# Order on ScalarE's queue: the clamp of w_out's third pair of pieces, the early up product's gelu, and the copies of the turned state reads

## The chip, the cores and the metric

The kernel runs on one core of a Trainium2 chip, in one launch. The metric is the device time in microseconds (us), the median of several runs. Engines are named as in the profile: PE is TensorE, DVE is VectorE, ACT is ScalarE, and PEld is TensorE's loading of weights.

## The reference

Block-recurrent cross attention (8 batches, 8 heads, 512 tokens, 32 state rows, 64 per head) is followed by a two-layer block with a quick gelu on 8 x 544 tokens, with a model width of 512 and an inner width of 2048. The weights w_in and w_out come as doubles, all else is float32.

```python
scores = scale * np.matmul(x, state.transpose(0, 1, 3, 2))
a = softmax(scores);   xread = np.matmul(a, state)
scores2 = scale * np.matmul(state, x.transpose(0, 1, 3, 2))
a2 = softmax(scores2); sread = np.matmul(a2, x)
x = concatenate([xread, sread], axis=2)      # then (B, H, S, D) -> (B*S, H*D)
h = x @ w_in
g = h * (1.0 / (1.0 + np.exp(-1.702 * h)))
return g @ w_out
```

## The kernel before

The order of every engine's work is written out by hand: an instruction is put on its engine's queue where the program calls for it, and semaphores settle the rest. Batches 0 and 1 are worked on together, while the weights come in; then the batches from 1 on take the steady route (`strassen_two`), each with the attention of the next one hooked in. Products with w_out use Strassen's seven products, P1 to P7.

**Rounding the weights.** w_in and w_out arrive in pieces (128 rows of 512 doubles, read as pairs of integer words), and are turned to float32 in pairs of pieces. A pair takes five steps on VectorE and two on ScalarE: the mask of the exponent bits (`pair_mask`, L305, into a part of `low`), the clamp of the exponents (`pair_clamp`, two relus on ScalarE in the same place, L225 and L226), the sign (L318, which reads the clamp's result), the low words (L319), the fraction (`pair_fraction`, L313), and the last product, which leaves the rounded pair in place (L322). `round_pair(j)` does the sign, the low words and the last product of pair j; `round_next(j)` slips the mask and the fraction of pair j + 1 between them, and then calls for the clamp of pair j + 1. Pairs 0 to 7 are w_in's, 8 to 15 are w_out's; pair 10 is w_out's third.

**The stage around the change.** It is the loop over eight slots i at the end of batch 0: in each slot the down products P1 to P7 of batch 0 gain one more part of their sums, from pair 8 + i. Their results stand in seven PSUM banks from the first slot to the last: P1, P6, P2 and P5 in the banks o_0 to o_3, P7 and P3 in the two banks of `psH`, and P4 in one of the two of `psA`. VectorE forms the sums of halves of w_out (`pair_sums`, into sums, t_room and w_out itself) and, in even slots, those of the activations (`left_sums`, into s_room). TensorE takes a slot's products in the order P1, P2, P6, P5, P7, P3, P4, each of four matmuls of 128x256; from the third slot on each slot also has one up product of batch 1 (four matmuls of 128x512) with its gelu (L659).

The first slot is different. After P1 it has the rest of batch 1's up matrices, the reads of the state by attention (`att_sread`), the sums of the first pair, `round_next(9)`, P2, one early up product of batch 1 (`up_x(1, f_early, dst=early)`, in a bank of `psH`, gelu to a room of xn, since its own room isn't free yet), the turning of the two batches' state reads (`att_srT`: a transpose on TensorE and a copy on ScalarE, L649, out of banks of `psA`), and P6, P5, P7, P3, P4. P3 is written to the bank that the early up product's gelu reads, and P4 to a bank that a copy of the turned state reads empties.

After the loop VectorE gathers the seven banks to batch 0's output (L1478, L1629) and makes sums that go out to DRAM (L1450). `strassen_two(1)` begins with P1 and P2 (L866), in between the scores of batch 2 (L456), which VectorE turns (L481); VectorE's first sum into osb (L873) frees the bank o_1 for the low-level products (L817), whose results ScalarE copies (L826).

Of the kernel before, what the change touches and what calls it, by code (L numbers as in the profile page):

```python
# [20 lines left out]
def kernel(  # L21
# [72 lines left out]
    def att_ps(shape, name):  # L94
        return psA.tile(shape, FP32, tag="att", name=name)
# [84 lines left out]
    PIECES = [("i", c, k) for c in range(NFC) for k in range(NPR)] + [("o", HF * k + (f + HF // 2) % HF) for f in range(HF) for k in range(2)]  # L180
# [43 lines left out]
    def clamp(sc):  # L224
        nc.scalar.activation(out=sc.bitcast(FP32), in_=sc, func=AF.Relu, bias=edge[0], scale=-8.0)  # L225
        nc.scalar.activation(out=sc, in_=sc.bitcast(FP32), func=AF.Relu, bias=edge[1], scale=-1.0)  # L226
# [67 lines left out]
    def pair_room(j):  # L294
        return low[:, 2 + 2 * j % 4 : 4 + 2 * j % 4].bitcast(I32)
# [7 lines left out]
    def pair_mask(j):  # L303
        load_weights(2 * j + 2)
        nc.vector.tensor_scalar(pair_room(j), pair_hi_lo(j)[0], 0x7FF00000, None, ALU.bitwise_and)  # L305

    def pair_clamp(j):
        clamp(pair_room(j))
        done["a"] = 2 * j + 2

    def pair_fraction(j):
        hi, _ = pair_hi_lo(j)
        nc.vector.tensor_scalar(pair_dst(j).bitcast(I32), hi, 0xFFFFF, 0x100000, ALU.bitwise_and, ALU.bitwise_or)  # L313

    def round_pair(j, *fills):
        hi, lo = pair_hi_lo(j)
        dst, sc = pair_dst(j), pair_room(j)
        nc.vector.scalar_tensor_tensor(sc, hi, -0x80000000, sc, ALU.bitwise_and, ALU.bitwise_or)  # L318
        nc.vector.scalar_tensor_tensor(dst, lo, 2.0**-32, dst.bitcast(I32), ALU.mult, ALU.add)  # L319
        for fn in fills:  # L320
            fn()
        nc.vector.scalar_tensor_tensor(dst, dst, 2.0**-20, sc.bitcast(FP32), ALU.mult, ALU.mult)  # L322
        done["b"] = 2 * j + 2
        raw.clear()
        refill()

    def round_next(j):
        round_pair(j, *((lambda: pair_mask(j + 1), lambda: pair_fraction(j + 1)) if 2 * j + 2 < len(PIECES) else ()))
        if 2 * j + 2 < len(PIECES):
            pair_clamp(j + 1)  # L330

    def piece(fill):
# [263 lines left out]
    def att_M(b, c, spare=False, banks=None, copied=True):  # L596

        m = mpool.tile([P, NG, FC], FP32, tag=f"M{turns['M'] % NFC if b < 2 else c}", name=f"M_{b}_{c}")
        turns["M"] += 1
        A[b]["M", c] = m  # L600
        name = f"M_{b}_{c}_"
        ps = banks or [
            psH.tile([P, FC], FP32, tag="h", name=name + str(g)) if spare else att_ps([P, FC], name + str(g)) for g in range(NG)
        ]
        by_state(b, ps, lambda rows, j: w_in[c][rows, j])
        M_banks[b, c] = ps
        if copied:
            M_copies(b, c)
# [15 lines left out]
    def eT_turn(b, g):  # L624
        t = A[b]["eT"][:, g].rearrange("p c q -> p (c q)")
        nc.vector.transpose(t, t)

    def att_sread(b):

        a = A[b]  # L630
        ps = att_ps([P, NG, D], f"sr_{b}")
        for g in range(NG):
            for c in range(SCH):
                for j in range(NPR):
                    st = slice(Ns * j, Ns * (j + 1))
                    e, v = a["eT"][:, g, j, Ns * c : Ns * (c + 1)], xn[b][:, NG * j + g, c]
                    nc.tensor.matmul(  # L637
                        ps[st, g], e, v,
                        start=(c == 0), stop=(c == SCH - 1),
                    )  # L640
        sr = apool.tile([P, P], FP32, tag="sr", name=f"sr_{b}", bufs=2)
        for g in range(NG):
            nc.scalar.activation(out=sr[:, D * g : D * (g + 1)], in_=ps[:, g], func=AF.Copy, scale=a["e2"][g][1])
        A[b]["sr"] = sr

    def att_srT(b):
        ps = att_ps([P, P], f"srT_{b}")
        nc.tensor.transpose(ps, A[b]["sr"], ident)
        nc.scalar.copy(srT[:, :, b, :], ps.rearrange("p (j n) -> p j n", j=NPR))  # L649
# [6 lines left out]
    def gelus(n):  # L656
        for _ in range(n):
            fn, kw = waiting.pop(0)
            fn(**kw)  # L659
# [728 lines left out]
    nin = NFC * NPR  # L1388
# [81 lines left out]
    def pieces(t, *shape):  # L1470
        n, k = shape
        return t.rearrange("p a b -> p (a b)").rearrange("p (n k t) -> p n k t", n=n, k=k)
# [17 lines left out]
    def a_of(f):  # L1490
        lo, hi = G[0, f // 2][:, f % 2], G[0, (HF + f) // 2][:, f % 2]
        return lo[:, :HS], hi[:, :HS], lo[:, HS:], hi[:, HS:]

    def t24(i):
        return t_room[i // 2][:, i % 2] if i < HF // 2 else T24[:, ORDER[i]]

    def turns_of(*lists):

        for step in zip(*lists):
            for fn, args in step:  # L1500
                fn(*args)

    def s_of(i):
        return tuple(v[:, i % 4] for v in s_rooms)

    def left_sums(i):

        u = ORDER[i] // 2
        (a11, a21), (a12, a22) = quarters(0, u, S), quarters(0, HF // 2 + u, S)
        s1, s2, *s4 = (v[:, i % 4 : i % 4 + 2] for v in s_rooms)  # L1510
        return [(tt, v) for v in ((s1, a21, a22, ALU.add), (s2, s1, a11), (a21, a11, a21), *((s, a12, s2) for s in s4))]
# [18 lines left out]
    def pair(i, *names):  # L1530

        f = ORDER[i]
        a11, a12, a21, a22 = a_of(f)
        s1, s2, s4 = s_of(i) if i >= 0 and names[0] not in ("P1", "P2") else (None,) * 3
        t = t24(i) if s1 is not None else None
        for name in names:
            lhs, rhs = {
                "P1": lambda: (a11, B11[:, f]),
                "P2": lambda: (a12, B21[:, f]),
                "P5": lambda: (s1, T1[:, f]),  # L1540
                "P6": lambda: (s2, t[:, 0]),
                "P7": lambda: (a21, B12[:, f]),
                "P3": lambda: (s4, B22[:, f]),
                "P4": lambda: (a22, t[:, 1]),
            }[name]()
            for r in range(2):
                nc.tensor.matmul(  # L1547
                    ps7[name][:, HN * r : HN * (r + 1)], lhs[:, P * r : P * (r + 1)], rhs,
                    start=(i == 0 and r == 0), stop=(i == HF - 1), skip_group_check=True,
                )  # L1550
# [10 lines left out]
    for i in range(HF):  # L1561
        if i > 1:
            round_next(nin // 2 + i)
        gelus(len(waiting))
        if i == 3:
            nc.scalar.copy(G[1, f_early // 2][:, f_early % 2], early)
        if i == 0:
            pair(i, "P1")
            att_M(1, 2, banks=bank_o[1::2])
            att_M(1, 3, True)  # L1570
            for b in (1, 0):
                for g in range(NG):
                    eT_turn(b, g)
            turns_of(left_sums(0))
            for b in (1, 0):
                att_sread(b)
            t_room.append(pieces(apool.tile([P, NG, SCH * P], FP32, tag="eT", name="t_room_1"), 2, 2))
            s_rooms.append(four(apool.tile([P, NG, NB * Ns], FP32, tag="e1", name="s4_room")))
            pair_sums(i, left_sums(0)[3:])
            round_next(nin // 2 + 1)  # L1580
            pair(i, "P2")
            f_early = rest.pop(0)
            early = xn[0].rearrange("p h c d -> p (h c d)")[:, :S]
            up_x(1, f_early, dst=early)
            att_srT(0)
            att_srT(1)
            pair(i, "P6")
            ps7["P7"], ps7["P3"] = (psH.tile([P, FC], FP32, tag="h", name=f"down_{k}") for k in (7, 3))
            ps7["P4"], up_bank = (att_ps([P, FC], f"down_{k}") for k in (4, "up"))
        else:  # L1590
            pair_sums(i)
            pair(i, "P1", "P2")
        if i == 2:
            G[1, f_early // 2] = free.pop(0)
        if i > 1 and i % 2 == 0:
            up_x(1, rest.pop(0), bank=up_bank, wait=True)
        if i == HF - 1:
            k1 = s_rooms[0][:, :2]
            nc.scalar.copy(k1, ps7["P1"].rearrange("p (r n) -> p r n", r=2))
        late()  # L1600
        if i > 1 and i % 2:
            up_x(1, rest.pop(0), bank=up_bank if i < HF - 1 else bank_o[0], wait=True)
        if i == HF // 2 + 1:
            load_state(2)
            load_x_squares(2)
# [140 lines left out]
```

## Time and profile before

| | |
|---|---|
| median of 3 runs | 692.15 us (691.82 to 692.54) |
| profiled execution | 690.55 us; its span 688.8 us, mean granted TensorE clock 0.995 |
| TensorE matmuls | busy 677.4 us, 98% of the span |
| VectorE | busy 555.1 us, 81% |
| ScalarE | busy 321.2 us, 47% |
| the chain that ended last | PE 93%, DMA 2%, DVE 2%, ACT 1% |

Times of instructions come from the profiled execution and count from its span's start; around the span lie 1.75 us more. A row of the timeline has its start, its length, the engine, the line of the kernel, the operation, out<-in by the names of tiles, and, where the engine stood idle before it, for how long and what ended that. The windows give the busy time of each engine in a stretch, then the granted clock.

### The profile page before, as it was taken

How to read it: one execution, taken by the hardware profiler on the slowest of the kernel's cores; microseconds unless marked ns; L12 is line 12 of the kernel's file. 1: busy time of each engine (PE TensorE's matmuls, PEld its weight loads, DVE VectorE, ACT ScalarE, POOL GpSimd, SP SyncE). 2: the span in 40 equal slices, each digit the busy share in tenths (PEclk: the TensorE clock that was granted, in tenths of full speed). 3: DMA queues.
4: the chain of work that ended last, by engine and by line, in shares of the span. 5: the costliest groups of instructions: out<-in, count | busy, mean ns of one | idle time of the engine just before them, and what ended most of it. 6: DMA issues, size and time to landing. Idle time of an engine off the chain costs nothing.

```text
span 688.8 us, 13508 instructions
## 1 busy us (share of the span) xinstructions
PE 677.4 (98%) x5339; PEld 578.4 (84%) x5339; DVE 555.1 (81%) x996; ACT 321.2 (47%) x697; POOL 1.4 (0%) x10
## 2 busy tenths in 40 slices
PE   8999899999999999999999999999999999999996
PEld 4444587779999899889988998989988998999995
DVE  5998899989999886988969796888688885886540
ACT  7799534124355543652365435554375237421410
POOL 0000000000000000000000000000000000000000
PEclk9999999999999999999999999999999999999999
DMA  9733436328353664247443755176425640251000
GB/s 319 300 112 78 179 127 165 111 108 262 106 122 112 192 192 117 42 147 206 139 81 96 212 155 109 34 197 194 119 33 156 198 147 9 76 168 48 1 2 30
DMA packets 102622, 89.48 MB, mean 130 GB/s; under 512 B 56736, under 2 KB 81824, under 8 KB 102560
## 3 DMA queue, kind: packets, MB, share of 16 engines
q1 hardware_dynamic: 102016, 88.50, 43.5%
q8 instruction: 42, 0.69, 0.4%
q14 instruction: 20, 0.16, 0.1%
q10 hardware_dynamic: 544, 0.13, 0.1%
HBM read 69.99 MB, written 18.61 MB: 129 GB/s over the span
## 4 chain that ended last, share of the span: by engine, by line
PE 93%; DMA 2%; DVE 2%; ACT 1%; issue 0%; DVEq 0%
PE low L817 28%; PE o L1227 15%; PE o L817 15%; PE upx L1227 6%; PE M L456 4%; PE o L1547 4%; PE h L670 4%; PE down L1547 3%; PE o L670 3%; PE o L716 3%; PE upw L1227 2%; PE o L866 2%; PE down_up L670 1%; PE o L456 1%; PE upx_sr L1227 1%; PE sr L637 1%
## 5 line engine op out<-in xcount | busy, mean ns | idle before, releaser
L817 PE MATMUL low<-w_out,g_room 128*128 128x128 f32 x416 | 54.3, 276 | 0.0
L817 PEld LDWEIGHTS low<-w_out,g_room 128*128 128x128 f32 x416 | 50.5, 192 | 4.5 <-issue 4.2
L1227 PE MATMUL o<-ta,M 128*128 128x256 f32 x192 | 49.9, 382 | 0.0
L1227 PE MATMUL upx<-aT,M 128*128 128x256 f32 x192 | 49.3, 379 | 0.0
L817 PE MATMUL low<-low,g_room 128*128 128x128 f32 x336 | 43.3, 275 | 0.0
L1227 PEld LDWEIGHTS o<-ta,M 128*128 128x128 f32 x192 | 35.5, 190 | 6.0 <-ACT g_room L1273 1.6
L817 PEld LDWEIGHTS low<-low,g_room 128*128 128x128 f32 x336 | 40.3, 192 | 0.0
L1227 PEld LDWEIGHTS upx<-aT,M 128*128 128x128 f32 x192 | 36.0, 190 | 4.6
L1233 ACT ACTIVATE g_room<-o 128x512 f32<-128x512 f32 (+1 forms) x56 | 31.4, 560 | 10.4 <-PE o L1227 10.4
L817 PE MATMUL low<-sums,later 128*128 128x128 f32 x272 | 34.9, 275 | 0.0
L594 ACT COPY M<-M 128x512 f32<-128x512 f32 x53 | 27.5, 596 | 15.0 <-PE M L456 15.0
L817 PEld LDWEIGHTS low<-sums,later 128*128 128x128 f32 x272 | 32.7, 192 | 0.1
L873 DVE TENSOR_TENSOR g_room<-g_room 128x512 f32<-128x512 f32 x48 | 31.7, 685 | 0.2
L1227 PE MATMUL o<-ta,ms 128*128 128x256 f32 x120 | 30.8, 379 | 0.0
L225 ACT ACTIVATE low<-low,edge 128x1024 f32<-128x1024 int32 (+1 forms) x18 | 19.1, 1062 | 23.5 <-DVE low L305 20.4
L1273 ACT COPY g_room<-o 128x512 f32<-128x512 f32 (+1 forms) x28 | 15.6, 555 | 25.3 <-PE o L1227 25.3
L1233 ACT ACTIVATE g_room<-g_room 128x512 f32<-128x512 f32 (+1 forms) x28 | 16.8, 600 | 20.8 <-DVE g_room L1236 20.8
L1227 PEld LDWEIGHTS o<-ta,ms 128*128 128x128 f32 x120 | 22.8, 190 | 3.1
L1227 PE MATMUL o<-aT,m 128*128 128x256 f32 x96 | 24.6, 379 | 0.0
L817 PEld LDWEIGHTS o<-w_out,g_room 128*128 128x128 f32 x160 | 19.4, 192 | 5.0 <-issue 5.0
L456 PE MATMUL M<-w_in,stT 64*32 64x512 f32 x344 | 23.2, 592 | 0.0
L873 DVE TENSOR_TENSOR g_room<-g_room,later 128x512 f32<-128x512 f32 x35 | 22.8, 683 | 0.0
(321 smaller groups left out, 1624.2 us busy)
## 6 DMA issues: line engine op xcount, KB each, us to landing
low<-low SPq DMA_DIRECT2D x108, 256.0 KB, 2.6
low<-low SPq DMA_DIRECT2D x11, 768.0 KB, 5.6
later<-in_moe_w_out_dram SPq DMA_DIRECT2D x16, 512.0 KB, 4.3
w_out<-in_moe_w_in_dram SPq DMA_DIRECT2D x12, 512.0 KB, 10.8
xsq<-in_x_dram SPq DMA_DIRECT2D x96, 64.0 KB, 2.3
xn<-in_x_dram SPq DMA_DIRECT2D x12, 512.0 KB, 4.3
squares<-e SPq DMA_DIRECT2D x32, 128.0 KB, 2.5
eT<-squares SPq DMA_DIRECT2D x8, 512.0 KB, 4.6
```

Source lines behind the costliest of these rows:

```text
L225: nc.scalar.activation(out=sc.bitcast(FP32), in_=sc, func=AF.Relu, bias=edge[0], scale=-8.0)
L456: nc.tensor.matmul(ps[g][st], state_of(b, NG * j + g, g), rhs(rows, j), start=True, stop=True)
L594: nc.scalar.copy(A[b]["M", c][:, g], ps)
L670: nc.tensor.matmul(hps, lhs[i], rhs[i], start=(i == 0), stop=(i == n - 1))
L716: nc.tensor.matmul(ps[:, r], lhs[f][:, P * r : P * (r + 1)], rhs[:, f], start=(first and r == 0 and f == 0), stop=(f == HF - 1), skip_grou ...
L817: nc.tensor.matmul(ps, lhs[f], rhs[:, f], start=(first and f == 0), stop=(f == QF - 1), skip_group_check=True)
L866: nc.tensor.matmul(ps[:, r], lhs[f][:, P * r : P * (r + 1)], rhs[:, f], start=(r == 0 and f == 0), stop=(f == HF - 1), skip_group_check=True,)
L873: nc.vector.tensor_tensor(out=out, in0=x0, in1=x1, op=op)
L1227: nc.tensor.matmul(ps[:, k], lhs[i][:, o : o + P], rhs[i], start=(first and k == 0 and i == 0), stop=(i == n - 1), skip_group_check=True,)
L1233: nc.scalar.activation(out=dst, in_=src, func=AF.Gelu_apprx_sigmoid)
L1273: nc.scalar.copy(c12, Y(u))
L1547: nc.tensor.matmul(ps7[name][:, HN * r : HN * (r + 1)], lhs[:, P * r : P * (r + 1)], rhs, start=(i == 0 and r == 0), stop=(i == HF - 1), s ...
```

## The change

`round_next` takes a second argument, with which its caller can leave the clamp of the next pair out. In the first slot the call for pair 9 uses it, and the clamp of pair 10 is called for after the early up product (whose gelu is put on ScalarE's queue there) and after both `att_srT`. ScalarE's order, before: clamp of pair 10 (two relus), gelu, copy, copy. After: gelu, copy, copy, clamp. The other engines' queues keep their order, and the DMAs too.

```diff
-    def round_next(j):
+    def round_next(j, clamped=True):
         round_pair(j, *((lambda: pair_mask(j + 1), lambda: pair_fraction(j + 1)) if 2 * j + 2 < len(PIECES) else ()))
-        if 2 * j + 2 < len(PIECES):
+        if clamped and 2 * j + 2 < len(PIECES):
             pair_clamp(j + 1)
...
             pair_sums(i, left_sums(0)[3:])
-            round_next(nin // 2 + 1)
+            round_next(nin // 2 + 1, False)
             pair(i, "P2")
             f_early = rest.pop(0)
             early = xn[0].rearrange("p h c d -> p (h c d)")[:, :S]
             up_x(1, f_early, dst=early)
             att_srT(0)
             att_srT(1)
+            pair_clamp(nin // 2 + 2)
             pair(i, "P6")
```

## The prediction, made before the changed kernel was run

> **What bounds the kernel now.** I read the page first: TensorE is busy for 98% of the span and VectorE for 81%, and the chain of work that ended last is 93% TensorE. A change on ScalarE (47%) matters only where TensorE waits for ScalarE. So the second view is the list of waits of TensorE's weight loads. Nearly all of it is issue gaps of 0.2 us; the largest single wait is this one (columns: total us, times, longest us):
>
> ```profile
> PEld down L1547 <- ACT xn L659: 2.7, 1, 2.7
> ```
>
> It happens once, and it is the wait that the diff touches: the gelu of the early up product (L659, out to xn) must leave its PSUM bank before the "P3" down product of the first slot can write there. The timeline of that stretch (start us, us, engine, line):
>
> ```profile
> 77.84 1.45 PE L670 MATMUL h<-low,M 128*128 128x512 f32 x3
> ...
> 80.78 0.68 DVE L305 TENSOR_SCALAR low<-later 128x1024 int32<-128x1024 int32 x1
> ...
> 81.07 1.03 PE L1547 MATMUL down<-w_out,g_room 128*128 128x256 f32 x4
> ...
> 81.50 1.15 ACT L225 ACTIVATE low<-low,edge 128x1024 f32<-128x1024 int32 x1 [4.03 <-DVE low L305]
> ...
> 82.68 1.15 ACT L226 ACTIVATE low<-low,edge 128x1024 int32<-128x1024 f32 x1
> ...
> 83.73 0.58 ACT L659 ACTIVATE xn<-h 128x512 f32<-128x512 f32 x1
> ...
> 84.21 0.42 ACT L649 COPY srT<-srT 128x128 f32<-128x128 f32 x2
> 84.36 0.83 PEld L1547 LDWEIGHTS down<-w_out,s_room 128*128 128x128 f32 x4 [2.67 <-ACT xn L659]
> 84.36 1.55 PE L1547 MATMUL down<-w_out,s_room 128*128 128x256 f32 x4 [2.27 <-ACT xn L659]
> ...
> 84.83 1.22 DVE L318 SCALAR_TENSOR_TENSOR low<-later,low 128x1024 int32<-128x1024 int32 x1
> ```
>
> See three things. The gelu's input was complete at 79.3 (77.84 + 1.45). ScalarE stood idle for 4.03 us up to 81.50, because the clamp in front of the gelu waits for VectorE's mask (L305, done 81.46). And VectorE takes the clamp's result only at 84.83, 1.0 us after it is there (82.68 + 1.15 = 83.83). The granted clock in the stretches after the wait (last three columns: PEclk, DMA share, GB/s):
>
> ```profile
> 84.00:85.00 1.00, 0.64 (x3) 0.59 (x4) 0.96 (x4) 0.64 (x3) 0.00 (x0) 0.97 0.73 299
> 85.00:86.00 1.00, 1.00 (x4) 0.81 (x3) 1.00 (x2) 0.00 (x0) 0.00 (x0) 0.50 0.03 12
> 86.00:87.00 1.00, 1.00 (x4) 0.72 (x4) 1.00 (x2) 0.00 (x0) 0.00 (x0) 0.50 0.00 0
> 87.00:88.00 1.00, 1.00 (x4) 0.81 (x3) 1.00 (x3) 0.18 (x1) 0.00 (x0) 0.50 0.00 0
> 88.00:89.00 1.00, 1.00 (x6) 0.83 (x5) 1.00 (x2) 0.97 (x1) 0.00 (x0) 0.83 0.83 201
> ```
>
> So the wait has a second price: about 3.4 us (84.9 to 88.3) at half clock.
>
> [...]the gelu sat ready from 79.3 to 83.73. [...]exchanging relus, gelu and copies needs no table load. The trace agrees: between L226 (relu, 82.68) and L659 (gelu, 83.73) no load stands.
>
> **The change part by part.** It removes and adds no instruction. Two relus of 1.15 us (L225, L226) move on ScalarE's queue behind one gelu (0.58) and two copies (0.42 together). No DMA is issued by the moved step; SP's and POOL's queues and VectorE's order stay.
>
> ScalarE after: its earlier work ends at 77.46 (76.50 + 0.96); the gelu runs 79.3 to 79.9; the copies need the transposes (79.12 + 0.38 = 79.50) and end by about 80.4. The mask is still done at 81.46, so the clamp still starts at 81.50 and ends at 83.83. For the clamp I take a cost of nothing: what hides it is that mask, 1.1 us later than ScalarE is free; without that cover another 1.0 us of slack stands before L318. Queued behind the clamp is then the next one (87.82), and that waits for VectorE's mask as before. VectorE's stream through this stage is thus unmoved.
>
> TensorE, the gain: four 128x256 matmuls take 0.865 us (starts 88.75, 89.61, 90.47, 91.34). P3 can follow at 81.07 + 0.865 = 81.93, not 84.36: **2.43 us**. P3, P4 and the next slot's P1 then need 3 x 0.865 at full clock, so that slot's P2 starts at 84.53, not 88.75: **4.22 us** in all, 1.79 of it from the half clock (3.41 x 0.5 = 1.71 is that, the rest start-up).
>
> What is late next: **VectorE's rounded pairs**. A slot is 7 x 0.865 = 6.05 us on TensorE, and 7.77 with an up product (1.72). Each slot's P1 needs its pair's last rounding step, L322, whose rows I read without waits before them: 81.98, 88.30, 96.67, 102.99, 111.35, 117.75, 125.02, each plus 1.22. Second slot: P1 at 83.66, pair ready 83.20. Third: 84.53 + 6 x 0.865 = 89.72, ready 89.52; weights load 0.2 earlier than their matmul, so this is a touch, 0.05. Fourth: 89.77 + 7.77 = 97.54, weights 97.33, ready 97.89 plus a hand-off of 0.04: 0.6 lost. The weights there loaded at 101.47, so the gain is **3.5 us** from here. Fifth: weights at 105.5 against 104.21; then 113.3 against 112.57, 121.0 against 118.97, 128.8 against 126.25. No further loss.
>
> Downstream: VectorE runs almost without a pause to 151.6, so it cannot follow at once. Its first waits that shrink are 0.50 (143.03, for a gelu) and the next:
>
> ```profile
> 154.10 1.31 DVE L481 STREAM_TRANSPOSE e<-o 128x512 f32<-128x512 f32 x2 [2.55 <-PE o L456]
> ...
> 159.32 0.69 DVE L873 TENSOR_TENSOR osb<-o,g_room 128x512 f32<-128x512 f32 x1 [0.23 <-PE o L866]
> ```
>
> With TensorE 3.5 earlier, VectorE comes to 154.10 at 154.10 - 0.50 - 2.55 = 151.05, TensorE's scores are there at 150.6, so VectorE gains 3.05. The 0.23 before osb goes too: 3.28. That osb frees bank o_1, which ScalarE's first copy of P5 (160.22) and through it TensorE need; TensorE had 0.15 us between that copy's end (160.58) and its next weights. So 3.28 to 3.5 comes through; I take **3.4**. From there all engines have moved together, and the later waits keep their lengths.
>
> Sum: the profiled execution took 690.55 (span 688.8, 1.75 around it) and becomes 687.15. The median of the runs, 692.15, lies 1.6 above it; less 3.4 it is **688.75**.
>
> Bounds of what the trace doesn't show. That TensorE now gets no half clock: if a window still falls, the gain is 1.7; if none does, 3.4; I take none, since idles of 0.84 us elsewhere (155.50, for issue) left PEclk at 1.00. [...]
>
> **The rivals.**
> (a) A half-clock window remains or returns at the fourth slot's 0.6 us: gain 3.4 - 1.7 = 1.7, time 690.45. Against it: the 0.84 us gaps.
> (b) VectorE's wait of 2.55 is not TensorE's alone (the scores' inputs or banks are late): then VectorE gains only 0.5 to 0.8 and osb holds TensorE to it; time 691.4, no change by measure. For it: VectorE at 81% has no other hole before 160. Against: the scores' squares were turned by 136.4 and their banks emptied by 138.8.
> (c) Slower: TensorE, no longer held by ScalarE, stops at VectorE's hand-offs instead, at third slot, fourth slot and osb, and each stop brings its half-clock window. Price: 4.2 - 0.7 of stops - 3 x 1.71 = a loss of 1.6, time 693.8. It decides from the third such window on. Against: the stops are 0.05, 0.6 and 0.2 us, and 0.84 did not do it.
> (d) The change doesn't do what it says: P3 also waits for something later than the gelu, P3's other inputs. VectorE's s_room was done by 77.9, so little speaks for it; time 692.15.
>
> **How the numbers follow.** Forecast 0.81, (a) 0.09, (b) 0.04, (c) 0.04, (d) 0.02. A measurement of this kernel can tell about 0.2%, 1.4 us, from no change. Faster by more than that: forecast and (a), 0.90; within it: (b) and (d), 0.06; slower: (c), 0.04. The forecast's own range is 687.9 (the whole 4.2 comes through) to 689.2; to hold 8 in 10 with the uncertainty of the sizes I let it reach into (a): 687.9 to 690.2.
>
> **What would show it.** In the changed profile: the gelu at 79.3 and both copies ahead of a clamp that still starts at 81.5; no wait of TensorE for L659 there; P3 near 81.9; PEclk 1.00 from 84 to 89; a wait of about 0.6 for L322 near 97.9; the 2.55 before L481 nearly gone. Wrong would be a clamp ending after 84.8, PEclk of 0.5 anywhere between 80 and 160, or a new TensorE wait of over 1 us before 165.

## The result, and the profile after

The changed kernel takes **688.27 us** (median of 4 runs, 687.59 to 688.36) against 691.99 (4 runs, 690.92 to 692.54) for the one before: 0.9946 of the time, 95% interval 0.9929 to 0.9963. That is 3.7 us less; 3.4 had been forecast. In two later sets, with more runs of the kernel before, the difference was 3.2 and 3.3 us. Its profiled execution took 688.34 (span 686.6), only 2.2 us less than the one shown of before; why these two differ by less than the medians is the first thing to read.

ScalarE in the timeline of the changed kernel:

```profile
79.29 0.60 ACT L659 ACTIVATE xn<-h 128x512 f32<-128x512 f32 x1 [2.06 <-PE h L670]
79.79 0.43 ACT L649 COPY srT<-srT 128x128 f32<-128x128 f32 x2
82.72 1.15 ACT L225 ACTIVATE low<-low,edge 128x1024 f32<-128x1024 int32 x1 [2.50 <-DVE low L305]
83.90 1.15 ACT L226 ACTIVATE low<-low,edge 128x1024 int32<-128x1024 f32 x1
```

The gelu starts the moment its bank is complete, the copies follow, and the clamp still starts when VectorE's mask (L305) is there. That mask is done at 82.7, though, not at 81.5. VectorE's transposes of batch 0's state squares (L626), first in the profile of before, then in this one with the mask:

```profile
73.24 1.31 DVE L626 STREAM_TRANSPOSE eT<-eT 128x512 f32<-128x512 f32 x2 [0.99 <-DMA eT<-squares]
```

```profile
74.47 1.30 DVE L626 STREAM_TRANSPOSE eT<-eT 128x512 f32<-128x512 f32 x2 [2.16 <-DMA eT<-squares]
...
82.00 0.68 DVE L305 TENSOR_SCALAR low<-later 128x1024 int32<-128x1024 int32 x1
```

TensorE of this execution:

```profile
81.04 1.03 PE L1547 MATMUL down<-w_out,g_room 128*128 128x256 f32 x4
81.90 1.03 PE L1547 MATMUL down<-w_out,s_room 128*128 128x256 f32 x4
82.77 1.03 PE L1547 MATMUL down<-t_room,sums 128*128 128x256 f32 x4
84.47 1.13 PE L1547 MATMUL o<-w_out,g_room 128*128 128x256 f32 x4 [0.68 <-DVE w_out L322]
```

P3 follows P7 at 81.90 (84.36 before). But the transfer of the squares landed later in this execution, L626 began at 74.47 instead of 73.24, and VectorE's whole stream through the stage is 1.2 us later (its mask starts at 82.00, 80.78 before). So TensorE meets VectorE at once, at the second slot. The list of the waits of TensorE's weight loads has no line for L659 with xn any more, and this one instead (total us, times, longest):

```profile
PEld o L1547 <- DVE w_out L322: 2.2, 3, 1.1
```

The granted clock (last but two) is whole where it was 0.50:

```profile
84.00:85.00 1.00, 0.53 (x2) 0.49 (x3) 0.93 (x3) 1.00 (x1) 0.00 (x0) 1.00 1.01 401
85.00:86.00 1.00, 1.00 (x6) 0.89 (x5) 0.96 (x3) 0.04 (x1) 0.00 (x0) 1.00 1.01 414
86.00:87.00 1.00, 1.00 (x7) 0.87 (x6) 1.00 (x2) 0.00 (x0) 0.00 (x0) 1.00 0.16 62
```

And downstream VectorE has no hole left, neither the 2.55 before L481 nor the 0.23 before osb:

```profile
152.10 1.30 DVE L481 STREAM_TRANSPOSE e<-o 128x512 f32<-128x512 f32 x2
...
156.99 0.68 DVE L873 TENSOR_TENSOR osb<-o,g_room 128x512 f32<-128x512 f32 x1
```

osb at 156.99 is 2.33 earlier than before. Add the 1.22 that VectorE started late, and it is 3.55, just above the 3.28 to 3.5 of the prediction. That the late start may be added in full is borne out by a second profile of the changed kernel (set 1 below): there L626 starts 0.80 earlier, osb 0.79 earlier (156.20), and the execution is 0.83 us shorter.

### The profile page after: what moved, and what is told of

It reads as the page before. It is cut to its first block, busy times and chain, and to the rows that moved or that the text cites. A ratio compares the mean times of both kernels' runs of the same rounds, so it can differ in the third digit from the quotient of the medians.

```text
span 686.6 us, 13508 instructions
## 1 busy us (share of the span) xinstructions
PE 675.9 (98%) x5339; PEld 577.1 (84%) x5339; DVE 554.5 (81%) x996; ACT 321.2 (47%) x697; POOL 1.5 (0%) x10
## 4 chain that ended last, share of the span: by engine, by line
PE 88%; DVE 5%; DMA 4%; ACT 2%; issue 0%; SPq 0%; DVEq 0%
PE low L817 28%; PE o L1227 15%; PE o L817 15%; PE upx L1227 6%; PE M L456 3%; PE h L670 3%; PE o L1547 3%; PE o L716 3%; PE upw L1227 2%; PE o L866 2%; PE down L1547 2%; PE o L670 2%; PE down_up L670 1%; PE o L456 1%; PE upx_sr L1227 1%; DMA out_dram<-osb_sr 1%
## 5 line engine op out<-in xcount | busy, mean ns | idle before, releaser
L456 PE MATMUL M<-w_in,stT 64*32 64x512 f32 x344 | 23.2, 592 | 0.0
```

The source lines that it names most:

```text
L456: nc.tensor.matmul(ps[g][st], state_of(b, NG * j + g, g), rhs(rows, j), start=True, stop=True)
```

## The experiments

All ratios are to the kernel before, with 95% intervals; kernels of one set ran on one chip and share the runs of before (medians there 690.91, 690.93 and 690.77).

| kernel | set | median us | ratio |
|---|---|---|---|
| before again | 1 | 690.62 | 0.9996 (0.9982 to 1.001) |
| changed, again | 1 | 687.69 | 0.9957 (0.9943 to 0.9971) |
| clamp_mid | 1 | 688.19 | 0.9969 (0.9957 to 0.998) |
| warm_wait | 1 | 689.57 | 0.9985 (0.9978 to 0.9993) |
| pad1 | 2 | 687.42 | 0.9947 (0.9929 to 0.9965) |
| pad4 | 2 | 689.8 | 0.9981 (0.9972 to 0.999) |
| sums_first | 2 | 686.63 | 0.9936 (0.9917 to 0.9955) |
| sums_only | 3 | 688.01 | 0.9963 (0.995 to 0.9975) |
| sums_first, again | 3 | 686.39 | 0.994 (0.9923 to 0.9957) |
| changed, third time | 3 | 687.5 | 0.9953 (0.9938 to 0.9969) |

**The kernel before, again (no edit).** Expected:

> The kernel before, unchanged: what two sets of runs of one kernel differ by, and a second profile of it. Theory A (the state-square transfers of batch 0, which VectorE waits for at about 73 us, land at different times from run to run, and everything behind them in this stage moves along): ratio 1.000 within 0.002; in this profile the transposes L626 of batch 0 start up to 1.3 us away from the first profile's 73.24, and the clamp, the gelu and P3 (84.36 there) move by the same amount. Rival B (the first profile is the rule): all within 0.1 us of the first profile.

It is its own equal in time. Its profile moved, as theory A said; VectorE and TensorE of it:

```profile
74.03 1.30 DVE L626 STREAM_TRANSPOSE eT<-eT 128x512 f32<-128x512 f32 x2 [1.27 <-DMA eT<-squares]
```

```profile
85.16 2.08 PE L1547 MATMUL down<-w_out,s_room 128*128 128x256 f32 x4 [3.03 <-ACT xn L659]
```

L626 is 0.79 later than in the first profile, and P3 0.80 later: in the old order the transfer's delay goes through mask, clamp and gelu straight into TensorE's wait, here 3.03 us. And the half clock now lasted 6.8 us (84.5 to 91.3) instead of 3.4:

```profile
87.00:88.00 1.00, 1.00 (x4) 0.80 (x3) 1.00 (x2) 0.00 (x0) 0.00 (x0) 0.50 0.00 0
88.00:89.00 1.00, 1.00 (x4) 0.82 (x3) 1.00 (x2) 0.39 (x1) 0.00 (x0) 0.50 0.18 20
89.00:90.00 1.00, 1.00 (x3) 0.75 (x3) 1.00 (x2) 0.97 (x2) 0.00 (x0) 0.50 0.79 172
```

That execution took 692.64. The kernel before spread over 688.85 to 693.43 in the 47 runs of this set; the changed one over 686.97 to 688.13 in 6. Every run also leaves its mean granted clock. It is 0.995 for the first profile of before, with one window of half clock, 3.4 us long (84.9 to 88.3), 0.993 for this one, with twice that, and 0.998 to 1.000 for all the profiles of this document without half clock. By these marks the 47 runs sort themselves:

| clock of the run | windows of half clock (estimate) | runs | us (median) |
|---|---|---|---|
| 0.998 to 1.000 | none | 15 | 688.85 to 690.52 (689.53) |
| 0.995 to 0.997 | one | 28 | 690.38 to 692.24 (691.18) |
| 0.993 | two | 4 | 692.04 to 693.43 (692.62) |

The number of windows is an estimate from the mean clock, by the two profiles with 3.4 us (0.995) and 6.8 us (0.993), and not read from each run's timeline; but the steps of 1.65 and 1.44 us fit a window, which costs about 1.7 by the prediction's count (half of its 3.41 us). So by this estimate the same kernel now meets no window, now one or two.

**The changed kernel, again (no edit), in sets 1 and 3.** Expected:

> The changed kernel, unchanged. Theory A: 3.4 to 3.8 us faster than before (ratio 0.9945 to 0.995); the profile shows no wait for the early gelu and PEclk 1.00 after it, and the waits for L322 at the second, third and fourth slots sum to 0.6 us when VectorE's L626 of batch 0 starts at 73.2, to 1.8 us when it starts at 74.5. Rival B (the 2.2 us between the two profiled executions are the true gain): ratio 0.997.

> The changed kernel once more, as the measure for the other two of this call: 3.2 to 3.7 us faster than before, ratio 0.9947 to 0.9955.

3.2 and 3.3 us faster by medians: 3.2 lies under the 3.4 to 3.8 of the first expectation, and 0.9957 just outside its ratios; rival B's 0.997 is at the very edge of set 1's interval (to 0.9971), and outside the first result's (to 0.9963) and set 3's (to 0.9969). The table above parts the 3.2 us of set 1: against the runs of before without a window (689.53) the changed kernel is 1.8 faster, and the other 1.4 are the windows. All 16 runs of the changed kernel have a clock of 0.998 or more.

In set 1's profile L626 stands at 73.67, and the waits of weight loads for L322 sum to 1.6 us (0.44, 0.41, 0.74 at the second, third and fourth slots). At 73.2 I had expected 0.6 in all, at 74.5 1.8; the 74.47 of the first profile had 2.2. By the starts of P1's matmuls TensorE lost 0.21, 0.18 and 0.51 us there, about 0.23 less each time: weight loads ran 0.2 ahead of their matmuls (82.40 and 82.61 for P4 just before the first of these waits).

**clamp_mid: the gelu ahead of the clamp, the copies behind it.**

```diff
+            pair_clamp(nin // 2 + 2)
             att_srT(0)
             att_srT(1)
-            pair_clamp(nin // 2 + 2)
```

> The changed kernel with the clamp between the gelu and the two copies of the turned state reads, so that only the gelu is ahead of it. P3 is free at 81.9 as in the changed kernel, but P4 waits for the first copy, which now comes behind the clamp, at about 84.2 with L626 at 73.2. Theory A: P4 waits 1.4 us; if that keeps the full clock, 2.8 us faster than before (ratio 0.996), and if it brings the half-clock window as well, 1.1 us faster (0.9984). Rival B (only the gelu matters, the copies could stay behind the clamp): as the changed kernel, 0.9946.

```profile
84.07 1.13 PE L1547 MATMUL down<-t_room,sums 128*128 128x256 f32 x4 [1.42 <-ACT srT L649]
```

P4 waits the 1.4 us expected, at full clock, and the kernel is 2.7 us faster than before by medians (2.8 expected); 0.5 slower than the changed one beside it, too little for the intervals to part. The copies do hold P4, but most of that wait is no loss: in this profile no wait for L322 follows, where the changed kernel has 1.6 us of them. For which of the two reasons TensorE stood mattered little here (0.5 us). The full clock is that of this profile: 4 of the 18 runs have a clock of 0.995 or 0.996 and take 689.93 to 690.97, the other 14 stay below 689. So this order brings a window in some runs.

**warm_wait: the old order, zeros multiplied in the wait.**

```diff
+    nought = konst.tile([P, FC], mybir.dt.bfloat16, name="nought")
+    nc.vector.memset(nought, 0.0)
...
             }[name]()
+            if i == 0 and name == "P3":
+                for _ in range(10):
+                    nc.tensor.matmul(ps7["P1"], nought[:, :P], nought, start=False, stop=False, skip_group_check=True)
             for r in range(2):
```

> The order of the kernel before, and in TensorE's wait for the gelu ten matmuls of 128x512 of zeros (about 2.1 us), which add nothing to P1's sums. The wait stays, the array is busy in it. Theory A (the wait costs 2.4 us itself and 1.7 to 1.8 us more through the half-clock window behind it): PEclk stays 1.00 and the kernel is 1.7 us faster than before (ratio 0.9975). Rival B (VectorE sets the pace right behind, so the half clock costs nothing): ratio 1.000. Rival C (zeros do not count as activity): PEclk 0.50 as before and 1.000.

The matmuls of zeros (L1550) are added to P1's bank. The lines of this kernel have moved: L1552 is L1547 of the others, L661 is L659.

```profile
81.54 2.32 PE L1550 MATMUL o<-nought 128*128 128x512 bf16 x10
84.52 1.13 PE L1552 MATMUL down<-w_out,s_room 128*128 128x256 f32 x4 [0.66 <-ACT xn L661]
```

P3 is as late as before, and the clock stays at 1.00 from 84 to 88, so that P2 of the second slot starts at 87.22, 2.70 after P3 (4.39 after it in the first profile of before). The kernel is 1.3 us faster by medians (1.7 expected), and its 22 runs lie within 688.94 to 690.42, with mean clocks of 0.997 to 1.000. So the half clock is real cost, rivals B and C fall, and the wide spread of the kernel before narrows with it. The median, 689.57, is that of the runs of before without a window (689.53 in this set), which fits: the zeros take the windows away and leave the rest as it was.

**pad1 and pad4: one and four relus more in front of the clamp.**

```diff
+            spare = xn[0].rearrange("p h c d -> p (h c d)")[:, S : 3 * S]
+            for _ in range(1):      # pad4: 4
+                nc.scalar.activation(out=spare, in_=spare.bitcast(I32), func=AF.Relu, bias=edge[0], scale=-8.0)
             pair_clamp(nin // 2 + 2)
```

> The changed kernel with one more relu of 1.15 us on ScalarE between the copies and the clamp (it works on a room that nobody reads). Theory A (the clamp waits for VectorE's mask, 1.1 us later than ScalarE is free, and VectorE takes its result 1.0 us late): nothing changes against the changed kernel, ratio to before 0.9946. Rival B (the clamp's start is critical): 1.1 us slower than the changed kernel, 0.996.

> The changed kernel with four such relus (4.6 us) between the copies and the clamp. Theory A: ScalarE is free at 85.0, the clamp ends at 87.3 where VectorE wants it at 84.83 (by a profile with L626 at 73.2): VectorE is held 2.5 us and TensorE with it at the third slot, so the kernel loses 2.5 us of the gain, 3.6 us if a half-clock window comes too: ratio to before 0.998 to 1.0. With L626 at 74.5 the mask is 1.2 us later and the loss 1.3 us: 0.9965. Rival B (VectorE has slack behind the clamp that takes it in): 0.9946.

In pad1 the clamp still waits for the mask (0.55 us are left of the cover), and the time is that of the changed kernel:

```profile
81.89 1.15 ACT L225 ACTIVATE low<-low,edge 128x1024 f32<-128x1024 int32 x1 [0.55 <-DVE low L305]
```

In pad4 VectorE waits for the clamp, and TensorE at the third slot for VectorE (a line of VectorE's waits, a row of TensorE's timeline, and the window right behind its wait):

```profile
DVE low L318 <- ACT low L226: 1.9, 1, 1.9
```

```profile
91.90 1.13 PE L1547 MATMUL o<-w_out,g_room 128*128 128x256 f32 x4 [1.97 <-DVE w_out L322]
```

```profile
92.00:93.00 1.00, 1.00 (x5) 0.90 (x6) 1.00 (x3) 0.48 (x1) 0.00 (x0) 1.00 1.04 426
```

It loses 2.4 us to pad1 (2.5 expected, or 1.3 with a late transfer). So the cost of nothing for the moved clamp was right, and its end is near. The last row shows full clock: 1.97 us of idling brought no half clock in this profile.

**sums_first: VectorE's first sums into the hole before batch 0's transposes, on top of the change.**

```diff
-            for b in (1, 0):
-                for g in range(NG):
-                    eT_turn(b, g)
+            for g in range(NG):
+                eT_turn(1, g)
             turns_of(left_sums(0))
+            for g in range(NG):
+                eT_turn(0, g)
```

> The changed kernel with VectorE's first three sums of activations (s_room, s_room, g_room; 1.9 us) put between the transposes of batch 1's and of batch 0's state squares (L626), where VectorE waits 1.0 us (2.2 in the second profile) for a transfer. Theory A (with the wait for the gelu gone, VectorE's rounding sets the pace of the first slots): VectorE comes 1.0 us earlier to every rounding, the waits of TensorE for L322 shrink from 0.6 us (1.8 in the profile of the changed kernel) to nearly nothing, and the kernel is 0.5 to 1.5 us faster than the changed one: ratio to before 0.9925 to 0.994. Rival B (the reads of the state, which need batch 0's squares, come later by 0.9 us and TensorE with them): no faster, 0.9945 to 0.996.

> sums_first once more, beside the changed kernel on one chip. Theory A: 0.8 to 1.2 us faster than the changed kernel. Rival (the 1.0 us between two calls came from the chip): within 0.4 us of it.

```profile
73.87 1.30 DVE L626 STREAM_TRANSPOSE eT<-eT 128x512 f32<-128x512 f32 x2
...
80.61 1.21 DVE L322 SCALAR_TENSOR_TENSOR w_out<-w_out,low 128x1024 f32<-128x1024 f32 x1
```

L626 of batch 0 no longer waits for its transfer, and the second slot's L322 starts at 80.61, against 82.27 to 83.20 in three profiles of the changed kernel. No wait of TensorE for L322 is left. 686.63 and 686.39 us: 0.8 us faster than pad1 and 1.1 us faster than the changed kernel in the same set. By medians this version beats both, in two sets. The intervals of the ratios overlap with the changed kernel's, and so do the single runs of one set (685.91 to 687.66 against 686.88 to 688.67), so the size of this gain is known only roughly.

**sums_only: the same edit of VectorE's order without the change.**

> The kernel before (clamp ahead of the gelu) with VectorE's three sums put between the transposes of batch 1 and batch 0, as in sums_first. Theory A (what made the wait for the gelu long was VectorE's mask at the head of ScalarE's queue; it comes 1.7 us earlier now): the clamp starts at about 80.1, the gelu at 82.3, P3 at about 82.9 instead of 81.9; TensorE waits 1.0 us or less and no half-clock window falls, so most of the gain comes without the change: 686.6 + 1.0 = 687.6, ratio to before 0.995. Rival B (the order on ScalarE is the only remedy): the gelu still comes near 83.7, and the ratio is 0.999 to 1.0.

```profile
82.31 1.03 PE L1547 MATMUL down<-w_out,g_room 128*128 128x256 f32 x4
84.85 1.13 PE L1547 MATMUL down<-w_out,s_room 128*128 128x256 f32 x4 [1.52 <-ACT xn L659]
```

2.8 us faster than before by medians, and half a us slower than the changed kernel: theory A's sum, with 0.4 more than its 687.6. The expected times in the profile missed, since in this execution batch 1's squares landed late (its L626 at 72.54; 70.7 to 71.5 in most others) and pushed the mask to 81.9. The wait is 1.52 us instead of 2.27 or 3.03, but not because the gelu came earlier: P3 starts at 84.85, later than the 84.36 of before. TensorE came later to the wait (P7 at 82.31, 81.07 before): by the times, its second read of the state (76.54, after idling for 0.56) waited for batch 0's transposes, which now stand behind the sums (L626 at 75.74). So this profile does not show theory A's earlier mask; what speaks for it are the ten runs, all with a clock of 0.998 or more, and 1.1 us below the three runs of before without a window in this set (median 689.09).

## Why the prediction was right

- **ScalarE's new order: right.** Gelu at 79.29 (79.3 forecast), copies done at 80.2 (80.4), no table load between (in this trace one takes 1.28 us; the nearest are at 64.43 and 154.45). The clamp starts with the mask, not with ScalarE; pad1 and pad4 show the cover and its end.
- **The 2.43 us at P3: right.** 81.90 in the profile, forecast 81.93.
- **The half-clock window, 1.7 to 1.8: right where one falls.** PEclk is 1.00 after the change. In the kernel before a run has none, one or two windows; they are worth 1.4 of the 3.2 us of set 1, and warm_wait, which removes them alone, gained 1.3. The prediction took the one window of its profile for the rule.
- **No window after the change: right, but one reason given for it does not hold.** The 0.84 us at 155.50 are a wait of weight loads; the matmuls before it (L456) run from 153.65 to 155.57 in the profile of before, so TensorE's matmuls did not pause there, and the full clock at that place said nothing of what idling brings. What the profiles show instead is that the waits which the change leaves (0.68 us of matmul idling at most in this stage) brought no window, in none of the three and by the clocks in none of the 16 runs.
- **VectorE is late next: right, if VectorE's times are those that were read.** The prediction found 0.6 us lost at the fourth slot, a touch at the third and none at the second. Counted in its way, by how late P1's matmuls start after the P4 before them, the three profiles of the changed kernel lost 1.5, 0.9 and 0.7 us: 0.5 at every fourth slot, 0.2 at every third, and at the second 0.84, 0.21 and 0.06, in step with the start of VectorE's mask (82.00, 81.20 and 81.06; 80.78 in the profile that was read). What the step left out is that the old order hangs on the same landing, through the mask and the clamp (in the two profiles of before L626 is 0.79 apart, P3 0.80): so, windows aside, a late landing costs both kernels about the same, and the difference stays. The first profile of the changed kernel had a landing 1.2 us later than that of before. That is why these two executions are only 2.2 us apart and the medians 3.2 to 3.7.
- **Two of the named signs of being wrong came true in the first profile:** a clamp ending after 84.8 (83.90 + 1.15 = 85.05), and a new TensorE wait of over 1 us (a weight load, 1.08 for L322). Both come from the late landing, not from the new order: in the two later profiles the clamp ends at 84.26 and 84.11, and the longest wait for L322 is 0.74.
- **Downstream, 3.28 to 3.5 come through: right.** VectorE's wait of 2.55 was TensorE's alone; it vanished, and rival (b) with it. Rivals (a) and (c) fall with the clock, and (d) with P3 at 81.90.
- **The difference was forecast, the time itself in part by luck.** 688.75 starts from the 692.15 of three runs. The 89 later runs of before have medians of 690.8 to 690.9 in their three sets, and the changed kernel's later medians, 687.7 and 687.5, lie just under 687.9, where the stated range begins.

## What to carry to other kernels

In the profile of before ScalarE took the gelu, whose input was complete at 79.3, only at 83.73, behind the clamp that stood ahead of it in the queue. Where that is so, an instruction that waits for a slow producer should not stand ahead of one whose input is ready and whose output frees a bank for the bound engine; ask what the first one waits for, not how long it runs. When such a wait is removed, find the engine that is late next and see whether its lateness comes from a hole of its own: filling that hole brought another 0.8 to 1.1 us here, by medians. And before a profile's gap of 0.05 or 0.2 us is counted as slack, look for a transfer upstream whose landing moves by 1 us from run to run, as that of the squares did here (L626 at 73.24 to 74.47).

## What was not expected of the hardware

How long TensorE must idle before the half clock comes has no single answer here. In one profile each the lengths do order the cases: 1.42, 1.52 and 1.97 us brought none, 2.27 one window of 3.4, 3.03 two (6.8). But by the clocks of the runs the same kernel falls on both sides: 15 of 47 runs of the kernel before had no window, and 4 of 18 runs of clamp_mid, with 1.42 us in its profile, had one. How long the wait was in those runs is not on record, and the landing of the squares moves it (in the two profiles of before, 0.79 us later went with 0.76 us more of waiting); so whether there is a border between 1.97 and 2.27, or whether something else decides, stays open. Ten matmuls of zeros (2.32 us) in the wait kept the clock whole: 1.00 from 84 to 88 in the profile of warm_wait.
